# Loading the first weights in halves, and a new order of the steps

## The chip, the cores and the metric

The kernel runs on one core of a Trainium2 chip. The metric is the device time of one execution in microseconds; it is the median of three runs: 506.88 us before the change (506.82 to 507.07). Engines are named as in the profile: PE is TensorE, DVE is VectorE, ACT is ScalarE, POOL is GpSimd, SP is SyncE, which here only issues DMAs.

## The reference

Three layers follow one another. The first is a chunked scan (batch 4, 8 heads, 768 positions, head size 32, state size 16), the second a dense layer with a leaky rectifier, the third a layer of 8 experts, where each token goes to one expert.

```
# scan, per chunk: L = exp(cum_i - cum_j) below the diagonal
y     = (C B^T * L) x + (C state) * exp(cum)
state = exp(sum log a) * state + sum_j B_j x_j exp(cum_end - cum_j)
x = y.transpose(0, 2, 1, 3).reshape(3072, 256)
# dense layer, 256 -> 2048 -> 256
h = x @ w_in;  x = max(0.01 * h, h) @ w_out
# experts: e = argmax(x @ w_gate + bias[modality])
out[mask_e] = softmax_e * (relu(x[mask_e] @ w1[e]) @ w2[e])
```

The weights `w_in` and `w_out` come as 64-bit floats: the kernel reads 8 bytes per element and rebuilds 32-bit floats on the chip.

## The kernel before, in words

The tokens are worked on in 24 chunks of 128 (the scan) and 6 blocks of 512 (the dense layer). Every large product is made of three in the `fp32r` type: the weight's rounded part times the data's rounded part, and the two cross products with the remainders. A *step* is a small function; its name in the plan has the chunk, block or piece as numbers:

- `load.c`, `lx.c`, `le.c`: the DMAs of chunk c. `load` (L419, L420) brings C and B, 1024 pieces of 64 bytes each; `lx` (L428) brings x; `le` (L438) brings the decays back from memory.
- `decay_a`, `decay_b`, `rows`, `high`, `out`, `cr`, `lows`, `lowv`, `end`, `fullmm`, `full`: the *decays' chain*, once, at the start: log of `a`, transposed on PE, summed by a triangular product (L351), copied to `cum` (L353), then laid out in rows.
- `bc.c.q`, `exp.c.q`: the decay matrices of the first chunks by PE and ACT. `trmm`, `trc`, `trb`, `trd`, `trde`, `cb`, `mul`, `p3`, `xa`, `xb`, `st`: the rest of the scan for chunk c: transposes, C times B (L549), times the decays on DVE (L558, L561), times x (L578 to L594), eviction to `xh` on ACT (L609) and its remainder `xl` on DVE (L615), the new state.
- `raw.i.k`, `raw.o.k`: the DMA of a quarter k of `w_in` (L656) or `w_out` (L672), 1 MB each. Each quarter is then converted in two halves: `hb` and `lb` on ACT (L634, L639), `or`, two instructions on DVE (L644, L645), which I call the *pair*, then `cast` on ACT and `subg` or `subv` (remainder) on POOL or DVE (L1188).
- `h.f` (six products, L694) with `sa`, `gg`, `gh`, `gl` on ACT, DVE, ACT, DVE; `y.f` (six products, L736): the dense layer, feature block f. `m1`, `m2`, `m2q` (L1070, L1101) do the same for the experts; `lg`, `l2`, `r1`, `rx`, `r2`, `r3`, `rp`, `be`, `put`, `yr`, `yc`, `ro` choose each token's expert and store rows.
- `warm.c.n`, `wy.n.1`: n products of zeros on PE, whose results are not used. `decay_a` has more of them inside.

The order is written out by hand: `PLAN` is a string of some 1,600 steps, and a loop calls them one by one. Each engine executes its own instructions in the order in which the plan issues them; between engines only data and buffers make an instruction wait. Some buffers that matter: two PSUM banks for `h`, three slots for raw weights, four for each of the chunk's inputs.

[...]

Of the kernel before, what the change touches and what calls it, by code (L numbers as in the profile page):

```python
# [27 lines left out]
    raw.o.0 exp.0.0 lx.0 cb.0 load.3 end high cd.1 bs.0 out warm.1.5 cr mul.0.0 hb.i.0.1 mul.0.2 trmm.1 lows trd.1
    trc.1 fullmm lb.i.0.1 lowv trde.1 or.i.0.1 bc.1.0 trb.1 lb.i.0.0 bc.1.1 exp.1.0 cumd or.i.0.0 lx.1 trmm.2 exp.1.1
    bc.2.0 full lx.2 cb.1 mul.0.1 cast.i.0.0 bs.1 cd.2 bc.2.1 cast.i.0.1 trc.2 subg.i.0.0 mul.1.1 p3.0 load.4 mul.1.0  # L30
    exp.2.1 mul.1.2 trb.2 subv.i.0.1 trd.2 xa.0 cb.2 cd.3 exp.2.0 st.0 le.4 trde.2 bc.3.1 bs.2 raw.i.1 xb.0 hb.o.0.0
    trmm.3 mul.2.1 lx.3 p3.1 mul.2.0 trb.3 hb.o.0.1 trc.3 load.5 mul.2.2 bc.3.0 xa.1 lb.o.0.0 st.1 trd.3 trde.3 xb.1
    or.o.0.0 exp.3.1 p3.2 exp.3.0 bs.3 cb.3 cast.o.0.0 cd.4 st.2 trmm.4 xa.2 mul.3.1 subg.o.0.0 wy.4.1 lb.o.0.1
    mul.3.0 trc.4 le.5 xb.2 trb.4 mask.4 mul.3.2 load.6 trd.4 trde.4 hb.i.1.0 p3.3 or.o.0.1 exp.4.0 xa.3 cd.5 trmm.5
    exp.4.1 xb.3 le.6 st.3 h.0 lx.4 lb.i.1.0 trc.5 raw.o.1 bs.4 mask.5 trb.5 cast.o.0.1 load.7 trd.5 h.1 sa.0 or.i.1.0
    trde.5 exp.5.0 cb.4 subv.o.0.1 sa.1 cast.i.1.0 gg.0 mask.6 hb.i.1.1 mul.4.2 h.2 lb.i.1.1 mul.4.0 subg.i.1.0
    mul.4.1 gh.0 gg.1 trmm.6 exp.5.1 p3.4 or.i.1.1 le.7 h.3 lx.5 xa.4 gl.0 gh.1 lx.6 sa.2 st.4 y.0 trb.6 cast.i.1.1
    trc.6 xb.4 hb.o.1.0 gl.1 sa.3 cb.5 bs.5 load.8 subv.i.1.1 exp.6.0 y.1 gg.2 mask.7 mul.5.0 gh.2 mul.5.1 load.9 h.4
    mul.5.2 lb.o.1.0 gl.2 exp.6.1 gg.3 p3.5 raw.i.2 or.o.1.0 gh.3 le.8 y.2 xa.5 le.9 sa.4 bs.6 lx.7 exp.7.0 cd.7 xb.5
    h.5 load.10 gl.3 gg.4 cb.6 sa.5 cast.o.1.0 y.3 mul.6.0 hb.o.1.1 gg.5 subg.o.1.0 gh.4 mul.6.1 trmm.7 mul.6.2  # L40
    lb.o.1.1 h.6 gh.5 gl.4 trb.7 or.o.1.1 exp.7.1 p3.6 sa.6 trc.7 h.7 bs.7 le.10 xa.6 gg.6 cast.o.1.1 raw.o.2 st.6
# [1247 lines left out]
```

## Time and profile before

| | us |
|---|---|
| median of three runs | 506.88 |
| the profiled execution, its own time | 507.78 |
| its span | 506.0 |
| PE busy | 491.9 (97%) |
| DVE busy | 324.3 (64%) |
| ACT busy | 284.9 (56%) |
| POOL busy | 130.4 (26%) |

The scan and the first two blocks of the dense layer begin together; the dense layer's products start at 31 us, the experts' products at 356 us, and the last product ends just before 499 us. The span of the profile is shorter than the execution's own time by 1.8 us, which lie around it. PE is "busy" while any product is in flight, so a busy PE can still lose time between products; starts of products tell more than the busy share.

### The profile page before, as it was taken

How to read it: one execution, taken by the hardware profiler on the slowest of the kernel's cores; microseconds unless marked ns; L12 is line 12 of the kernel's file. 1: busy time of each engine (PE TensorE's matmuls, PEld its weight loads, DVE VectorE, ACT ScalarE, POOL GpSimd, SP SyncE). 2: the span in 40 equal slices, each digit the busy share in tenths (PEclk: the TensorE clock that was granted, in tenths of full speed). 3: DMA queues.
4: the chain of work that ended last, by engine and by line, in shares of the span. 5: the costliest groups of instructions: out<-in, count | busy, mean ns of one | idle time of the engine just before them, and what ended most of it. 6: DMA issues, size and time to landing. Idle time of an engine off the chain costs nothing.

```text
span 506.0 us, 8845 instructions
## 1 busy us (share of the span) xinstructions
PE 491.9 (97%) x3250; PEld 392.2 (78%) x3252; DVE 324.3 (64%) x702; ACT 284.9 (56%) x627; POOL 130.4 (26%) x131
## 2 busy tenths in 40 slices
PE   8889999999999999999999999999999999999994
PEld 5556787776777777777777778788899989989894
DVE  3999989978768666676667854577772536335330
ACT  6898878855556735564566434654543564354331
POOL 2140215100040302030101103072035448063054
PEclk9999999999999999999999999999999999999998
DMA  8999860051626096136200271018026746050012
GB/s 196 200 214 230 249 157 2 1 88 22 122 54 107 1 101 130 47 25 135 78 1 2 47 258 44 0 29 120 23 40 149 251 147 218 35 169 2 0 59 74
DMA packets 102454, 48.40 MB, mean 96 GB/s; under 512 B 84065, under 2 KB 93698, under 8 KB 102402
## 3 DMA queue, kind: packets, MB, share of 16 engines
q1 hardware_dynamic: 99330, 41.35, 36.8%
q0 software_dynamic: 3072, 6.41, 4.1%
q8 instruction: 27, 0.44, 0.4%
q14 instruction: 25, 0.20, 0.1%
HBM read 41.14 MB, written 6.60 MB: 94 GB/s over the span
## 4 chain that ended last, share of the span: by engine, by line
PE 63%; issue 17%; POOL 7%; DVE 4%; DMA 4%; ACT 4%; POOLq 1%; SPq 0%; ACTq 0%
PE y L736 25%; PE h L694 25%; POOL out_dram L1131 4%; PE cb L549 2%; PE psy L591 2%; POOL w2s L1044 2%; DMA il<-ids,pi 2%; POOL xg L1022 1%; PE psy L586 1%; DMA xt<-in_x_dram 1%; PE hp L1070 1%; ACT e L460 1%; DVE gl L716 1%; PE yr L897 1%; PE lp L779 1%
## 5 line engine op out<-in xcount | busy, mean ns | idle before, releaser
L701 ACT ACTIVATE sa<-h 128x512 f32<-128x512 f32 x96 | 57.5, 598 | 58.8 <-PE h L694 58.6
L706 DVE TENSOR_TENSOR gg<-sa,h 128x512 f32<-128x512 f32 x96 | 65.2, 681 | 26.2 <-ACT sa L701 25.6
L694 PE MATMUL h<-xh,wih 128*128 128x512 f32 x192 | 79.1, 412 | 1.7 <-ACT xh L609 0.9
L716 DVE TENSOR_TENSOR gl<-gg,gh 128x512 fp32r<-128x512 f32 x96 | 67.1, 702 | 19.8 <-ACT gh L711 18.4
L736 PE MATMUL y<-gh,woh 128*128 128x512 f32 x192 | 79.2, 412 | 0.0
L736 PE MATMUL y<-gl,woh 128*128 128x512 f32 x192 | 75.3, 392 | 0.2
L694 PE MATMUL h<-xl,wih 128*128 128x512 f32 x192 | 75.2, 392 | 0.0
L736 PE MATMUL y<-gh,wol 128*128 128x512 f32 x192 | 75.1, 391 | 0.0
L694 PE MATMUL h<-xh,wil 128*128 128x512 f32 x192 | 75.0, 391 | 0.0
L711 ACT CAST gh<-gg 128x512 fp32r<-128x512 f32 x96 | 59.1, 619 | 21.5 <-DVE gg L706 18.2
L1088 DVE SCALAR_TENSOR_TENSOR hl<-hp,hh 128x512 fp32r<-128x512 f32 x48 | 33.1, 690 | 58.4 <-ACT hh L1084 58.4
L1101 PE MATMUL o<-w2s,hh 128*128 128x256 f32 x384 | 70.3, 282 | 0.0
L1070 PE MATMUL hp<-x2h,w1s 128*128 128x512 f32 x192 | 67.3, 396 | 0.1
L1101 PEld LDWEIGHTS o<-w2s,hh 128*128 128x128 f32 x384 | 61.8, 190 | 3.1
L1084 ACT ACTIVATE hh<-hp 128x512 fp32r<-128x512 f32 x48 | 28.6, 599 | 61.3 <-PE hp L1070 51.8
L1101 PE MATMUL o<-w2s,hl 128*128 128x256 f32 x192 | 54.1, 282 | 0.0
L460 ACT ACTIVATE e<-e,ncum 128x128 f32<-128x128 f32 x160 | 50.8, 397 | 0.0
L442 POOL TENSOR_SCALAR_AFFINE_SELECT e<-e 128x1024 f32<-128x1024 f32 x20 | 22.9, 1150 | 102.4 <-DMA e<-cumd 78.0
L694 PEld LDWEIGHTS h<-xh,wih 128*128 128x128 f32 x192 | 36.2, 188 | 15.5 <-issue 3.6
L880 POOL DMA_INDIRECT il<-ids,pi x24 | 25.9, 1077 | 81.6 <-DVE base L871 59.0
L736 PEld LDWEIGHTS y<-gh,woh 128*128 128x128 f32 x192 | 36.1, 188 | 10.6 <-issue 3.3
L694 PEld LDWEIGHTS h<-xh,wil 128*128 128x128 f32 x192 | 36.0, 188 | 7.9
(227 smaller groups left out, 805.2 us busy)
## 6 DMA issues: line engine op xcount, KB each, us to landing
r<-in_moe_w_dram SPq DMA_DIRECT2D x24, 512.0 KB, 4.8
e<-cumd SPq DMA_DIRECT2D x20, 512.0 KB, 4.4
raw<-in_moe_w_in_dram SPq DMA_DIRECT2D x4, 1024.0 KB, 6.2
raw<-in_moe_w_out_dram SPq DMA_DIRECT2D x4, 1024.0 KB, 6.5
...
ct<-in_C_dram SPq DMA_DIRECT2D x24, 64.0 KB, 4.8
bt<-in_B_dram SPq DMA_DIRECT2D x24, 64.0 KB, 3.8
```

Of the source, the lines that this page charges most:

```text
L460: s.activation(out=e[:, h, :], in_=i, func=AF.Exp, bias=ncum[:, cc, b * H + h:b * H + h + 1])
L694: t_.matmul(h, lhsT=w[:, k, fs], rhs=xx[:, k, :], start=(i == 0), stop=(i == 5))
L701: s.activation(out=d["sa"], in_=d["h"], func=AF.Copy, scale=0.01)
L706: v.tensor_tensor(out=d["gg"], in0=d["sa"], in1=d["h"], op=ALU.max)
L711: s.copy(out=d["gh"], in_=d["gg"])
L716: v.tensor_tensor(out=gl, in0=d["gg"], in1=d["gh"].bitcast(F32), op=ALU.subtract)
L736: t_.matmul(y_t[j][k], lhsT=w[:, f, ds], rhs=gg, start=(f in first and i == 0), stop=(f in last and i == 2))
L880: w = g.indirect_dma_start(out=il[:], out_offset=IndirectOffsetOnAxis(ap=pi[:, q:q + 1], axis=0), in_=ids[:, c0 + q:c0 + q + 1], in_offset ...
L1070: t_.matmul(d["hp", f], lhsT=d[1][:, k, part, fs], rhs=xx[:, k, :], start=(n == 0), stop=(n == 5))
L1084: s.activation(out=e_h(i, f, "hh"), in_=ex[i]["hp", f], func=AF.Relu)
L1088: v.scalar_tensor_tensor(out=e_h(i, f, "hl"), in0=d["hp", f], scalar=0.0, in1=d["hh", f].bitcast(F32), op0=ALU.max, op1=ALU.subtract)
L1101: t_.matmul(d["o", q], lhsT=d[h, f][:, q * P:(q + 1) * P], rhs=d[2][:, f, part, :], start=(start and n == 0), stop=(f == NF2 - 1 and n == ...
```

## The change

1. A quarter of a weight is loaded by two DMAs of 512 KB in place of one of 1 MB: `raw.i.k.kk` brings 128 of 256 rows, `raw.o.k.q` half of the rows. The buffer is still one for both halves. There are 16 such DMAs in place of 8. The first half of `w_in`'s first quarter is issued straight behind `a`, ahead of the first chunk's C and B.
2. Products of zeros: the three in `decay_a` (L355, 256 columns) and the five of `warm.1.5` (512 columns) go; `wy.4.1` behind the transposes of chunk 4 becomes `wy.6.1`. Twelve such products become six (the six at the very start and the two at L346 and L347 stay).
3. The plan is in another order from end to end. It has the same steps otherwise.

```diff
 PLAN = """
-    load.0 raw.i.0 kg1 load.1 decay_a kvb bc.0.1 kvc decay_b bc.0.0 exp.0.1 load.2 trmm.0 hb.i.0.0 rows trc.0 trb.0
+    raw.i.0.0 load.0 kg1 load.1 decay_a hb.i.0.0 bc.0.1 load.2 lb.i.0.0 decay_b kvb bc.0.0 exp.0.1 kvc or.i.0.0
...
@@ def decay_a():
         v.tensor_copy(cum.rearrange("p c r -> p (c r)"), p1[:, 0:NCB * BH])
-        for _ in range(3):
-            t_.matmul(p0[:, 256:512], lhsT=zer[:, 0:P], rhs=zer[:, 0:256], start=True, stop=True)
         dk["cum"] = cum
...
-    def load_win(k):
-        r = rawp.tile([P, 2, 512], w_in.dtype, tag="raw", name="raw")
-        nc.sync.dma_start(out=r, in_=w_in[:, k * 512:(k + 1) * 512].rearrange("(k p) f -> p k f", p=P))
-        raws["i", k] = r
+    def load_win(k, kk):
+        if kk == 0:
+            raws["i", k] = rawp.tile([P, 2, 512], w_in.dtype, tag="raw", name="raw")
+        nc.sync.dma_start(out=raws["i", k][:, kk, :], in_=w_in[kk * P:(kk + 1) * P, k * 512:(k + 1) * 512])
...
-    def load_wout(k):
-        r = rawp.tile([P, 4, DM], w_out.dtype, tag="raw", name="raw")
-        nc.sync.dma_start(out=r, in_=w_out[k * 512:(k + 1) * 512, :].rearrange("(k p) f -> p k f", p=P))
-        raws["o", k] = r
+    def load_wout(k, q):
+        if q == 0:
+            raws["o", k] = rawp.tile([P, 4, DM], w_out.dtype, tag="raw", name="raw")
+        o = k * 512 + 2 * q * P
+        nc.sync.dma_start(out=raws["o", k][:, 2 * q:2 * q + 2, :], in_=w_out[o:o + 2 * P, :].rearrange("(k p) f -> p k f", p=P))
```

What this moves on the engines is shown at two places. First SP, from its first DMA on (`ct` and `bt` are C and B of a chunk, `xt` is x). Before:

```order
L1157 DMA a_sb<-in_a_dram 96x256
L419 DMA ct<-in_C_dram 128x8x16
L420 DMA bt<-in_B_dram 128x8x16
L656 DMA raw<-in_moe_w_in_dram 128x2x512
L419 DMA ct<-in_C_dram 128x8x16
L420 DMA bt<-in_B_dram 128x8x16
L419 DMA ct<-in_C_dram 128x8x16
L420 DMA bt<-in_B_dram 128x8x16
L672 DMA raw<-in_moe_w_out_dram 128x4x256
L428 DMA xt<-in_x_dram 128x8x32
```

After:

```order
L1157 DMA a_sb<-in_a_dram 96x256
L656 DMA raw<-in_moe_w_in_dram 128x512
L418 DMA ct<-in_C_dram 128x8x16
L419 DMA bt<-in_B_dram 128x8x16
L418 DMA ct<-in_C_dram 128x8x16
L419 DMA bt<-in_B_dram 128x8x16
L418 DMA ct<-in_C_dram 128x8x16
L419 DMA bt<-in_B_dram 128x8x16
L656 DMA raw<-in_moe_w_in_dram 128x512
L418 DMA ct<-in_C_dram 128x8x16
L419 DMA bt<-in_B_dram 128x8x16
L673 DMA raw<-in_moe_w_out_dram 128x2x256
```

The first half quarter of `w_in` now stands ahead of all chunks' C and B, the second half behind those of three chunks; half a quarter of `w_out` stands where a whole one stood.

Second DVE, behind the copy of `cum` and some constants (`hb<-hb,lb` and `hb<-raw,hb` are the pair of a half quarter; `cumb` is the last step of the decays' chain that `bc.1` waits for). Before:

```order
L496 TENSOR_TENSOR cm<-ps,par 128x256
L400 COPY cend<-p__264 32x2
L400 COPY cend<-p_251 32x4
L450 TENSOR_TENSOR cd<-ct,ecum 128x128
L538 TENSOR_TENSOR bs<-bt,e 128x128
L380 TENSOR_TENSOR cr<-p_251,cumb 64x512
L558 TENSOR_TENSOR e<-e,cb 128x256
L561 TENSOR_TENSOR e<-e,cb 128x512
L496 TENSOR_TENSOR cm<-ps,par 128x256
L387 TENSOR_TENSOR cumb<-cr,cumb 32x512
L644 SCALAR_TENSOR_TENSOR hb<-hb,lb 128x512
L645 SCALAR_TENSOR_TENSOR hb<-raw,hb 128x512
```

After:

```order
L643 SCALAR_TENSOR_TENSOR hb<-hb,lb 128x512
L644 SCALAR_TENSOR_TENSOR hb<-raw,hb 128x512
L495 TENSOR_TENSOR cm<-ps,par 128x256
L537 TENSOR_TENSOR bs<-bt,e 128x128
L449 TENSOR_TENSOR cd<-ct,ecum 128x128
L399 COPY cend<-p__274 32x2
L399 COPY cend<-p_261 32x4
L379 TENSOR_TENSOR cr<-p_261,cumb 64x512
L557 TENSOR_TENSOR e<-e,cb 128x256
L449 TENSOR_TENSOR cd<-ct,ecum 128x128
L557 TENSOR_TENSOR e<-e,cb 128x256
L386 TENSOR_TENSOR cumb<-cr,cumb 32x512
```

The pair of the first half stands ahead of chunk 0's `cm` now. Before, two pairs followed the instruction that writes `cumb`, one behind the other (the first ends the rows shown); after, only one pair stands near that place.

In the dense layer's stretch, from the first `h` to the last `y`, the plan interrupts the `h` and `y` steps with shorter PE steps 77 times in place of 80, with the same 102 short steps.

## Rows read from the trace of the kernel before

**Rows 1.** Section 1 of the page: busy time, share, instructions.

```profile
PE 491.9 (97%) x3250; PEld 392.2 (78%) x3252; DVE 324.3 (64%) x702; ACT 284.9 (56%) x627; POOL 130.4 (26%) x131
```

**Rows 2.** Busy us (count) of PE, PEld, DVE, ACT, POOL by stretch; granted clock, DMA share, GB/s.

```profile
0.00:10.00 10.00, 8.61 (x56) 5.83 (x59) 3.16 (x14) 5.41 (x11) 3.59 (x18) 1.00 0.80 158
...
20.00:30.00 10.00, 8.84 (x117) 5.35 (x118) 9.45 (x26) 7.82 (x21) 2.45 (x2) 1.00 0.99 242
30.00:40.00 10.00, 8.95 (x65) 6.04 (x66) 9.17 (x20) 10.00 (x30) 3.79 (x3) 1.00 0.95 238
...
50.00:75.00 25.00, 25.00 (x165) 19.45 (x166) 21.79 (x40) 20.69 (x47) 4.18 (x3) 1.00 0.75 216
```

**Rows 3.** PE's waits: total us, times, longest.

```profile
PE h L694 <- DVE gg L706: 0.9, 3, 0.4
...
PE rp L849 <- DVE ohb L827: 0.6, 1, 0.6
PE yr L897 <- ACT cdt L529: 0.4, 1, 0.4
```

**Rows 4.** Timeline of the opening: start, duration, instruction [idle before <- what ended it].

```profile
1.27 0.42 SPq L419 DMA_DIRECT2D ct<-in_C_dram  x1
...
4.87 0.21 ACT L341 ACTIVATE tab<-tab 1x8 f32<-1x8 f32 x1
...
6.75 0.28 DVE L273 TENSOR_TENSOR gm<-mask 128x128 f32<-128x128 f32 x1
...
9.09 0.69 ACT L634 ACTIVATE hb<-raw 128x512 f32<-128x512 f32 x1
...
9.39 0.42 DVE L496 TENSOR_TENSOR cm<-ps,par 128x256 f32<-128x256 f32 x1 [2.20 <-PE ps L491]
...
15.19 0.69 DVE L644 SCALAR_TENSOR_TENSOR hb<-hb,lb 128x512 int32<-128x512 int32 x1
```

**Rows 5.** Section 6 of the page: DMA issues, size, median us to landing.

```profile
raw<-in_moe_w_in_dram SPq DMA_DIRECT2D x4, 1024.0 KB, 6.2
...
ct<-in_C_dram SPq DMA_DIRECT2D x24, 64.0 KB, 4.8
```

**Rows 6.** Timeline, products of zeros and what stands behind them.

```profile
1.27 2.74 PE L1153 MATMUL wps<-zer 128*128 128x512 bf16 x6 [1.27 <-DVE tab L1150]
...
5.64 0.85 PE L355 MATMUL p<-zer 128*128 128x256 bf16 x3
...
11.48 1.03 PE L1165 MATMUL bc<-zer 128*128 128x512 bf16 x4 [0.16 <-issue]
...
13.44 0.33 PE L490 MATMUL ps<-ident,ct 128*128 128x128 f32 x1 [0.93 <-DVE e L558]
```

**Rows 7.** Timeline ahead of the first product of the dense layer.

```profile
30.82 0.36 ACT L609 CAST xh<-psy 128x256 fp32r<-128x256 f32 x1
...
31.23 0.50 PE L694 MATMUL h<-xh,wih 128*128 128x512 f32 x1 [0.88 <-ACT xh L609]
```

**Rows 8.** Timeline, a short step inside the dense layer's stream.

```profile
270.33 0.39 PE L736 MATMUL y<-gh,wol 128*128 128x512 f32 x1
270.65 0.71 PE L549 MATMUL cb<-cm,btt 32*128 32x256 f32 x8
271.29 0.50 PE L694 MATMUL h<-xh,wih 128*128 128x512 f32 x1
271.63 0.40 PE L694 MATMUL h<-xl,wih 128*128 128x512 f32 x1
```

**Rows 9.** Timeline, a stall inside the stream.

```profile
232.26 1.09 POOL L442 TENSOR_SCALAR_AFFINE_SELECT e<-e 128x1024 f32<-128x1024 f32 x1 [10.23 <-PE psy L594]
...
233.42 0.39 PE L736 MATMUL y<-gh,wol 128*128 128x512 f32 x1
...
234.21 0.50 PE L694 MATMUL h<-xh,wih 128*128 128x512 f32 x1 [0.41 <-DVE gg L706]
```

**Rows 10.** One line of DVE: count, ns min/median/max, first and last start us.

```profile
L835 DVE TENSOR_SCALAR sm<-sm x6: 170/170/906, 145.1 to 365.6; 128x4 f32<-128x4 f32 x6
```

More of the change, by code (lines that the diff above doesn't have):

```diff
@@ L26 @@
 PLAN = """
-    load.0 raw.i.0 kg1 load.1 decay_a kvb bc.0.1 kvc decay_b bc.0.0 exp.0.1 load.2 trmm.0 hb.i.0.0 rows trc.0 trb.0
[L28 to L41, printed above, removed]
@@ L117 @@
-    m1.5.2 re.5.1 rl.5.1 m2.4.5 re.5.2 rl.5.2 m1.5.3 m1.5.4 re.5.3 oe.3.1 rl.5.3 re.5.4 m1.5.5 sh2.5.0 rl.5.4 m2.4.6
-    oe.3.0 re.5.5 sc.3.0 rl.5.5 m1.5.6 sl2.5.0 sc.3.1 m1.5.7 re.5.6 sc.3.2 rl.5.6 m2.4.7 re.5.7 sc.3.3 rl.5.7 oe.4.2
-    m2q.5.0 oe.4.3 oe.4.1 oe.4.0 sc.4.0 m2q.5.1 sc.4.1 sc.4.2 m2q.5.2 sc.4.3 oe.5.1 oe.5.0 sc.5.0 sc.5.1 m2q.5.3
-    oe.5.2 sc.5.2 oe.5.3 sc.5.3
+    raw.i.0.0 load.0 kg1 load.1 decay_a hb.i.0.0 bc.0.1 load.2 lb.i.0.0 decay_b kvb bc.0.0 exp.0.1 kvc or.i.0.0
+    raw.i.0.1 trmm.0 exp.0.0 load.3 rows trc.0 trb.0 cast.i.0.0 bs.0 cd.1 subg.i.0.0 cb.0 end high raw.o.0.0 out cr
@@ new lines @@
+    lx.0 mul.0.0 lows fullmm cd.2 mul.0.1 hb.i.0.1 cumd lowv trmm.1 lx.1 full trd.1 trc.1 lb.i.0.1 bc.1.0 mul.0.2
+    trde.1 bc.1.1 or.i.0.1 trb.1 exp.1.0 trmm.2 raw.o.0.1 exp.1.1 cb.1 lx.2 trc.2 hb.o.0.0 bc.2.1 bs.1 cd.3 trb.2
+    mul.1.0 lb.o.0.0 trd.2 mul.1.2 p3.0 exp.2.1 load.4 or.o.0.0 cast.i.0.1 bc.2.0 xa.0 trde.2 xb.0 bc.3.1 exp.2.0
+    mul.1.1 subv.i.0.1 cast.o.0.0 trmm.3 cb.2 st.0 exp.3.1 le.4 bs.2 subg.o.0.0 trc.3 hb.o.0.1 lx.3 p3.1 mul.2.0 trb.3
+    mul.2.2 raw.i.1.0 mul.2.1 bc.3.0 xa.1 load.5 xb.1 trd.3 exp.3.0 cb.3 st.1 trde.3 bs.3 p3.2 cd.4 lb.o.0.1 mul.3.2
@@ new lines @@
+    mul.5.2 h.4 mask.7 sa.3 mul.5.0 gh.2 gg.3 lx.7 exp.6.1 p3.5 gl.2 cd.7 lx.8 h.5 xa.5 gh.3 xb.5 exp.7.1 load.9 bs.6
+    gl.3 cb.6 sa.4 y.2 mul.6.1 lb.o.1.0 mul.6.0 le.8 mul.6.2 sa.5 raw.o.1.1 trmm.7 gg.4 load.10 y.3 trb.7 exp.7.0
+    trc.7 or.o.1.0 p3.6 gg.5 trd.7 xa.6 h.6 gh.4 xb.6 trde.7 st.6 cast.o.1.0 bs.7 gl.4 raw.i.2.0 cb.7 gh.5 le.9
+    subg.o.1.0 h.7 raw.i.2.1 mul.7.2 hb.o.1.1 raw.o.2.0 mul.7.1 lb.o.1.1 gl.5 le.10 y.4 sa.6 raw.o.2.1 mul.7.0
+    or.o.1.1 sa.7 load.11 p3.7 gg.7 trmm.8 gg.6 xa.7 y.5 cast.o.1.1 xb.7 gh.6 subv.o.1.1 h.16 gl.6 gh.7 cd.8 gl.7
@@ new lines @@
+    te1 yr.3.1 xb.21 y.69 gl.70 yc.3.1 sa.71 sa.72 gg.71 cb.22 gg.72 gh.71 y.70 mul.22.0 gl.71 r3.3 h.73 gh.72
+    mul.22.2 mul.22.1 y.71 gl.72 sa.73 te2 yr.3.0 h.74 yc.3.0 gg.73 ro.3 lx.23 trmm.23 sa.74 p3.22 gh.73 exp.23.0
+    gl.73 y.72 st.22 trb.23 xa.22 gg.74 h.75 trc.23 gh.74 te3 y.73 sa.75 gl.74 ix.0 h.76 gg.75 w1.0 trd.23 sa.76 y.74
+    ix.1 trde.23 gh.75 gg.76 w2.0 xb.22 h.77 gh.76 bs.23 gl.75 cb.23 sa.77 h.78 gg.77 gl.76 mul.23.0 y.75 sa.78
+    mul.23.1 gg.78 h.79 mul.23.2 p3.23 sa.79 gh.77 y.76 ga.1 xa.23 xb.23 gl.77 h.80 gh.78 gl.78 y.77 gg.79 sa.80 gg.80
@@ L121 @@
+    m2.4.5 re.5.3 dr sl2.5.1 rl.5.3 m1.5.4 m1.5.5 re.5.4 rl.5.4 m2.4.6 re.5.5 rl.5.5 m1.5.6 m1.5.7 re.5.6 rl.5.6
+    m2.4.7 re.5.7 rl.5.7 oe.4.2 m2q.5.0 oe.4.0 oe.4.1 sc.4.0 sc.4.1 m2q.5.1 oe.5.0 oe.4.3 sc.4.2 sc.4.3 m2q.5.2 oe.5.1
+    sc.5.0 sc.5.1 m2q.5.3 oe.5.2 sc.5.2 oe.5.3 sc.5.3
 """
@@ L1202 @@
         "trde": tr_de, "cb": cb_mm, "bs": cb_bs, "mul": cb_mul, "p3": p3_mm, "xa": p3_xa, "xb": p3_xb, "st": p3_st,
-        "raw": lambda t, k: (load_win if t == "i" else load_wout)(k),
+        "raw": lambda t, k, q: (load_win if t == "i" else load_wout)(k, q),
         "h": lambda f: h_mm(f // NF, f % NF), "sa": lambda f: h_sa(f // NF, f % NF), "gg": lambda f: h_gg(f // NF, f % NF),
```

150 lines of the change are left out of this document (75 added, 75 removed).

## The prediction

> **What bounds the kernel now.** I read the busy times first, then the same by stretch, then PE's waits, then the timeline where the waits are. PE is busy for 491.9 us of the span of 506.0 [rows 1], and from 50 us on it fills every stretch, while DVE and ACT still have time over [rows 2]. So whatever the change does behind 50 us can only come from PE's own sequence: how closely product follows product. The opening is different. Between 20 and 40 us DVE is busy for 9.45 and 9.17 of each 10 us and ACT for 10.00 of the second ten, while PE loses more than one microsecond in each [rows 2]. PE then waits 0.88 us for ACT's `xh` (from 30.82 us) before the first dense product, which starts at 31.23 us [rows 7]. So the opening ends when DVE and ACT have worked through their lists; the DMA queue is full beside them (share 0.99 from 20 to 30 us), but no wait of PE ends on a landing there. What the kernel can win is bounded: the opening, the waits inside PE's stream, and the joints between products.
>
> **The change part by part.** The number of products, evictions and conversions is the same but for the zeros, so I price places.
>
> *The first pair in an idle place.* Before, DVE stands idle for 2.20 us ahead of chunk 0's `cm` at 9.39 us, from the end of the constants at 7.2 us on (9.39 - 2.20; the last row before it begins at 6.75) [rows 4]. The pair of `w_in`'s first half ran at 15.19 us, at 0.69 us an instruction, so 2 x 0.69 = 1.38 us, in the stretch that DVE fills. The change puts it into the idle place. Can the data be there? Its DMA is issued second, in the place where C of chunk 0 stood, at 1.27 us [rows 4]. A full megabyte takes 6.2 us to land [rows 5] and a half cannot take longer in an emptier queue, so it lands by 7.5 us; half the 6.2 gives 4.4 us. ACT needs `hb` and `lb`, 0.69 us each by the row of `hb` (1.4 us), and has nothing else from 5.08 us on (4.87 plus 0.21) but the exponential of `cum`, until the first decay matrix is there [rows 4]. The pair can then begin between 6.5 and 9.3 us. At the early end it is done before `cm` could start; at the late end it delays `cm` by 1.3 us, which takes all of the gain back. I take the early end, since by the rows DMA serves half a megabyte first. DVE's list ahead of the first dense product is then 1.38 us shorter, and ACT's by the same 1.4 us: -1.4 us. If PE's part of the opening moves too (next paragraph), at most 0.8 more: -2.2.
>
> *Behind the half.* Chunk 0's C and B now stand behind 512 KB. They took 4.8 us to land in a loaded queue [rows 5]; another 1.6 us, a quarter of 6.2, brings them to 8 us at the latest, and the transposes that read them end at about 9.4 us [rows 4]. I cost it at nothing; if that cover is gone, each microsecond of lateness is one on the chain. The scan's loads behind it gain, since half a quarter of `w_out` and half of `w_in` stand ahead of x of chunk 3 where whole ones stood. SP issues eight DMAs more; with the DMA engines at 0.99 [rows 2] it is the queue and not SP that sets the pace: nothing.
>
> *The zeros.* The three at L355 take 0.85 us on PE ahead of the first decay matrix, 0.64 us of it start to start (0.21 each) [rows 6]. The five of `warm` fill a time in which PE waits anyway: behind them it is still idle for 0.93 us until DVE has the first product ready [rows 6]. Their removal is worth nothing. The two added ones cost 2 x 0.22 = 0.43 us, by the row of the four at 11.48 us (1.03 us less the last one's flight of 0.38, over three); they stand behind chunk 4's transposes, where DVE's list is the limit. Both ends: -0.64 (the chain moves up by all three) to +0.43. I take 0 and leave both ends in the range.
>
> *Joints.* In the stream a product follows the last after 0.23 us. Around one short step the row before it and the row behind it start later: 270.65 - 270.33 = 0.32, 271.63 - 271.29 = 0.34 [rows 8], so 0.09 + 0.11 = 0.2 us for each interruption. Three fewer: -0.6 us (-0.3 to -0.9, as the kinds of steps differ).
>
> *Waits inside the stream.* PE waits 0.9 us in three places for `gg`, 0.6 for `rp` and 0.4 for `yr`: 1.9 us in five places [rows 3]. The starts lose more than the idle time shows: 234.21 - 233.42 = 0.79 where 0.23 is the pace, so 0.56 against 0.41 idle [rows 9]. With 0.15 more for each of five: 1.9 + 0.75 = 2.65 us. The row in front explains the one at 234.21: DVE's L835 on 4 numbers took 906 ns once and 170 ns otherwise [rows 10], and in that time POOL ran an affine select, 1.09 us from 232.26 [rows 9]. Such a delay hits PE only where the plan leaves `gg` little time. A `y` has six or more large steps between it and its `h` in 43 of 96 cases, in the old order in 37: a little more room. I expect a third of the 2.65 back, -0.9 us, with ends -2.65 (all gone) and +1.0 (all stay, and two more of 0.5).
>
> The Trainium skill, SBUF — State Buffer, section "Who interferes with whom", says that GpSimd and VectorE hold a shared pair of ports exclusively, whoever came first, and that a plain `tensor_scalar` can be among them. The 906 ns agree with it. By that rule the waits are tied to the number of such meetings, and POOL has the same instructions as before; then this term is 0, the sum -2.0 and the time 504.9.
>
> Sum: -1.4 - 0.6 - 0.9 = -2.9 us. The profiled execution took 507.78 us (its span of 506.0 and 1.8 around it) and would take 504.9; it stands 0.90 above the median of the three runs, and from that median, 506.88, I get **504.0 us**. The low end adds -2.2 - 0.9 - 2.65 = -5.75: 501.1. The high end, +0.43 - 0.3 + 1.0 = +1.1: 508.0. What lies behind the last product I leave as it is: the last steps are the same.
>
> **The rivals.**
>
> *The gain of the opening is swallowed.* Behind 31 us ACT is full for ten microseconds (10.00 of 10 [rows 2]); if the dense layer's start is early but its evictions come no earlier, PE waits there instead. For it: ACT's row. Against: ACT's list is shorter by the same 1.4 us. The time: joints alone, 506.88 - 0.6 = 506.3.
>
> *PE's clock.* In the opening the six first zero products start about 0.43 us apart ((2.74 - 0.58) / 5, taking 0.58 as the last one's flight), the three at 5.64 us with half the columns 0.21; at 11.48 us the full ones start 0.22 apart [rows 6]. So PE rises from 1.2 to 2.4 GHz between 6 and 11 us, after an unbroken run of products since 1.27 us; the column of the granted clock reads 1.00 all the time and does not show it [rows 2]. If without the three zeros the rise fails to come in the opening's first part, the decay matrices, rows and transposes take twice as long: between the zeros that end at 6.49 and those at 11.48 us lie 5.0 us [rows 6], at the busy share of 0.86 [rows 2] 4.3 us of work. Then the first term is +4.3 in place of -1.4: +4.3 - 0.6 - 0.9 = +2.8, 509.7. Each microsecond at the lower level costs half a microsecond, so it decides over the 2.9 us of the forecast if the rise comes later than 6.5 + 2 x 2.9 = 12.3 us. Against: the decay matrices move up into the zeros' place and keep PE as busy. The Trainium skill, TensorE: Matmul & The Clock Gate, section "Part 1: The HAM clock gate (the "warmup" mystery)", says that the slow state is the default, that activity lifts it, and that where the rise falls varies from run to run. It speaks against taking products of zeros out, and the rise in the rows agrees with it.
>
> *The waits stay.* The order of before is good already and the new one has as many meetings of POOL and DVE: -1.4 - 0.6 = -2.0, 504.9. It lies inside the forecast's own side.
>
> *New waits.* If the new order has twice as many (+2.65) and the half lands late (0): 506.88 + 2.65 - 0.6 = 508.9.
>
> **How the numbers follow.** Two tenths of a percent, 1.0 us, is about what a measurement can tell from no change here. Forecast (faster, 501 to 505.8, the waits that stay among it): 0.70. Swallowed (506.3, no change): 0.16. Clock: 0.07. New waits: 0.07, of both together 0.13 slower and 0.01 about the same. So faster 0.70, same 0.17, slower 0.13. The range is 501.2 to 507.2: it leaves the two slower rivals out, about 0.13, and little below.
>
> **What would show it.** In the new profile the first pair (`hb` on DVE) stands between 6.5 and 9 us and `cm` starts no later than 9.5; the first dense product starts at 29.8, not 31.2 (29.0 to 31.6); PE's waits for `gg`, `rp` and `yr` sum to 1.3 or less; from the first dense product to the last expert product it takes some 1.5 us less than before. I am wrong if the first dense product stays at 31, if the first decay matrices' products start at twice their distance beyond 8 us, or if PE's waits inside the stream are 2 us or more.

## The result and the profile after

The changed kernel takes 511.05 us (median of 5 runs, 509.49 to 511.34) where the kernel before takes 506.88 (505.93 to 507.68). The ratio is 1.0074, with a 95% interval of 1.0060 to 1.0088: slower by some 3.8 us by the ratio, where I had predicted 504.0. The profiled execution took 510.19 us, with a span of 508.5 us (before: 507.78 and 506.0). It lies 0.9 us below its median and the one of before 0.9 above, so the two traces show only 2.4 of the 4.2 us between the medians.

The place to begin is the same as before: how busy TensorE is. Section 1 of the page of the changed kernel:

```profile
PE 491.9 (97%) x3246; PEld 393.5 (77%) x3246; DVE 332.4 (65%) x702; ACT 285.7 (56%) x627; POOL 131.3 (26%) x131
```

PE's record has four instructions fewer and is busy for the same 491.9 us [rows 1]; a product that runs slowly counts as busy too. DVE has the same 702 instructions, and they take 8.1 us more in all. Both say: look at the waits and at durations that have changed. PE's waits in the changed kernel (us in total, times, longest):

```profile
PE psy L590 <- DMA xt<-in_x_dram: 2.6, 1, 2.6
...
PE l L793 <- DVE lt L786: 1.1, 1, 1.1
...
PE o L1101 <- DVE hl L1088: 0.7, 1, 0.7
```

The waits for `gg`, `rp` and `yr`, 1.9 us in [rows 3], are gone, and these three stand in their place. The timeline of the changed kernel shows the opening, and then the first of the three:

```profile
5.62 0.67 ACT L633 ACTIVATE hb<-raw 128x512 f32<-128x512 f32 x1 [0.54 <-DMA raw<-in_moe_w_in_dram]
...
7.03 0.68 DVE L643 SCALAR_TENSOR_TENSOR hb<-hb,lb 128x512 int32<-128x512 int32 x1
...
8.35 0.42 DVE L495 TENSOR_TENSOR cm<-ps,par 128x256 f32<-128x256 f32 x1
...
29.86 0.48 PE L694 MATMUL h<-xh,wih 128*128 128x512 f32 x1
...
147.75 0.37 SPq L419 DMA_DIRECT2D bt<-in_B_dram  x1
...
148.17 5.52 SPq L427 DMA_DIRECT2D xt<-in_x_dram  x2
...
161.13 0.64 PE L590 MATMUL psy<-e,xt 128*32 128x128 f32 x16 [2.58 <-DMA xt<-in_x_dram]
...
162.67 0.63 PE L694 MATMUL h<-xl,wih 128*128 128x512 f32 x1
...
163.09 0.63 PE L694 MATMUL h<-xh,wil 128*128 128x512 f32 x1
```

The opening did what was forecast: the first pair runs on DVE at 7.03 us, `cm` follows at 8.35, and the first dense product starts at 29.86 us instead of 31.23 [rows 7]. Much later, x of chunk 13 is issued at 148.17 us (the first of the two `xt` of that row), behind a load of B that SP issues only at 147.75, and it lands 12.8 us later; PE stands still for 2.58 us. Behind that wait the products follow each other at 0.42 us (163.09 - 162.67) instead of 0.23. The reason is the granted clock, the share of 2.4 GHz that PE gets: the column behind the five engines in the same kernel's busy times by stretch.

```profile
12.00:14.00 2.00, 1.69 (x6) 0.80 (x7) 1.94 (x6) 1.78 (x4) 0.00 (x0) 0.53 0.66 129
14.00:16.00 2.00, 2.00 (x17) 1.28 (x15) 1.85 (x3) 1.48 (x5) 0.00 (x0) 0.62 1.12 289
...
160.00:162.00 2.00, 0.87 (x26) 0.79 (x27) 0.02 (x1) 0.00 (x0) 0.00 (x0) 1.00 0.66 154
162.00:164.00 2.00, 2.00 (x14) 1.63 (x13) 1.30 (x4) 1.67 (x5) 0.00 (x0) 0.57 0.99 183
164.00:166.00 2.00, 2.00 (x7) 1.59 (x6) 1.79 (x10) 1.22 (x2) 0.00 (x0) 0.57 0.97 271
```

From 162.3 to 165.7 us PE runs at 1.2 GHz, just behind a pause; so the late load costs its 2.6 us and about 1.6 more in this trace. From 12 to 16 us the clock is low too, where the zero products stood before.

The other two waits are on DVE. Its line L1044 makes the *remainders* of the expert weights, what the rounded parts leave over. First before, then the changed kernel (ns min/median/max), then the single ones that were stretched:

```profile
L1044 DVE TENSOR_TENSOR w1s<-r,w1s x12: 1206/1218/1292, 334.6 to 466.7; 128x1024 fp32r<-128x1024 f32 x12
```

```profile
L1044 DVE TENSOR_TENSOR w1s<-r,w1s x12: 1214/1221/4128, 330.3 to 464.7; 128x1024 fp32r<-128x1024 f32 x12
...
L1044 POOL TENSOR_TENSOR w2s<-r,w2s x6: 2392/2408/2423, 359.3 to 485.1; 128x1024 fp32r<-128x1024 f32 x6
```

```profile
359.34 2.39 POOL L1044 TENSOR_TENSOR w2s<-r,w2s 128x1024 fp32r<-128x1024 f32 x1 [25.09 <-ACT w2s L1040]
359.62 3.19 DVE L1044 TENSOR_TENSOR w1s<-r,w1s 128x1024 fp32r<-128x1024 f32 x1
...
401.15 4.13 DVE L1044 TENSOR_TENSOR w1s<-r,w1s 128x1024 fp32r<-128x1024 f32 x1
401.76 2.42 POOL L1044 TENSOR_TENSOR w2s<-r,w2s 128x1024 fp32r<-128x1024 f32 x1
...
450.06 3.83 DVE L1044 TENSOR_TENSOR w1s<-r,w1s 128x1024 fp32r<-128x1024 f32 x1 [0.25 <-ACT w1s L1040]
450.38 2.42 POOL L1044 TENSOR_TENSOR w2s<-r,w2s 128x1024 fp32r<-128x1024 f32 x1
```

Three of these twelve run while GpSimd works on the same line, and each takes about its 1.22 us and the time the two lie beside each other; GpSimd's keep their 2.4 us. In the kernel before no two of them meet. `lt` and `hl` stand in DVE's list behind the first two, and PE waits for them; behind the third nothing waits.

The last place is the end. From the start of the last group of products to the end of the span it was 10.1 us before and is 11.3 now, and the program's last waits on GpSimd (L1235) spread out. First the changed kernel, then the one before (first and last start in us):

```profile
L1235 POOLq EVENT_SEMAPHORE  x5: 17/43/43, 504.1 to 506.4; - x5
```

```profile
L1235 POOLq EVENT_SEMAPHORE  x5: 17/43/43, 502.7 to 503.0; - x5
```

The five waits began within 0.3 us of each other and now begin within 2.3: GpSimd pauses for 2.1 us among them (504.2 to 506.3 us), and in that pause a load on a queue of instructions runs, at 504.7 us.

Starts of the same work in the two traces and in four kernels below (timeline, us):

| start of | before | changed | x13_early | lows_apart | splice140 | x13_dve |
|---|---|---|---|---|---|---|
| first dense product | 31.23 | 29.86 | 31.55 | 31.95 | 30.43 | 29.77 |
| dense product `h`, block 2, step 0 | 140.82 | 136.35 | 138.14 | 138.53 | 138.37 | 136.57 |
| block 4, step 0 | 251.40 | 249.61 | 247.20 | 251.51 | 249.56 | 245.93 |
| last dense step | 357.90 | 356.83 | 354.43 | 358.74 | 356.10 | 353.15 |
| expert slot 3 | 424.97 | 426.30 | 423.72 | 425.85 | 423.17 | 420.83 |
| last product group | 495.85 | 497.17 | 494.59 | 496.71 | 494.05 | 491.69 |
| end of the span | 505.98 | 508.47 | 506.16 | 508.65 | 503.98 | 501.83 |

The changed kernel is 4.47 us ahead at 141 us, and 2.49 behind at the end. It loses 2.7 us between 141 and 251, 0.7 to 358, 2.4 to 425 and 1.2 in the tail (each is the change of the difference between the two columns).

### The profile page after: what moved, and what is told of

The parts are those of the page before. It is cut to its first block, busy times and chain, and to the rows that moved or that the text cites. A ratio compares the mean times of both kernels' runs of the same rounds, so it can differ in the third digit from the quotient of the medians.

```text
span 508.5 us, 8885 instructions
## 1 busy us (share of the span) xinstructions
PE 491.9 (97%) x3246; PEld 393.5 (77%) x3246; DVE 332.4 (65%) x702; ACT 285.7 (56%) x627; POOL 131.3 (26%) x131
## 4 chain that ended last, share of the span: by engine, by line
PE 83%; issue 4%; DMA 3%; DVE 3%; SPq 2%; POOL 1%; ACT 1%; POOLq 0%; DVEq 0%
PE y L736 26%; PE h L694 25%; PE hp L1070 11%; PE o L1101 10%; PE psy L590 3%; DMA xt<-in_x_dram 3%; PE cb L548 2%; POOL out_dram L1131 1%; PE psy L585 1%; PE yr L897 1%; DVE w1s L1044 1%; PE xps L1051 1%; SPq L418 1%; DMA cumd<-cumrow 1%; PE lp L779 1%
## 5 line engine op out<-in xcount | busy, mean ns | idle before, releaser
L716 DVE TENSOR_TENSOR gl<-gg,gh 128x512 fp32r<-128x512 f32 x96 | 68.6, 717 | 14.6 <-ACT gh L711 13.8
L441 POOL TENSOR_SCALAR_AFFINE_SELECT e<-e 128x1024 f32<-128x1024 f32 x20 | 24.4, 1228 | 110.3 <-DMA e<-cumd 75.8
L694 PEld LDWEIGHTS h<-xh,wih 128*128 128x128 f32 x192 | 36.4, 189 | 10.4 <-issue 2.5
```

The costliest lines, as they stand in the source:

```text
L694: t_.matmul(h, lhsT=w[:, k, fs], rhs=xx[:, k, :], start=(i == 0), stop=(i == 5))
L716: v.tensor_tensor(out=gl, in0=d["gg"], in1=d["gh"].bitcast(F32), op=ALU.subtract)
```

## The experiments

Each group of runs had its own runs of the kernel before: 506.8, 509.4, 506.7, 509.8 and 510.0 us. So the ratio to these counts; one thousandth is half a microsecond. The changed kernel has 1.0074 from its first runs, with which the first two groups are compared. In the third group (put0_late, which turned out to be the same order) it had 1.0090, in the fifth (pair_after) 1.0128: the loss itself differs from group to group, by more than the smaller steps below.

**First group (506.8): one suspect each.**

x13_early. The load goes back to where it stood before, which is 131.58 us in this trace (131.98 before):

```diff
- ... l2.1 gh.34 y.33 lx.13 gl.34 ...
+ ... p3.10 ... load.15 trc.11 st.10 lx.13 trb.11 ...
```

> The changed kernel with one load moved: x of chunk 13 is issued where the kernel before issues it, right behind the store of chunk 10, and no longer behind the bias-table load that waits for chunk 13's decays. Theory A (the late load costs the 2.66 us that the product psy of chunk 13 waits for xt, and the 1.6 us that the dense products behind it lose at 1.2 GHz): the kernel takes 511.05 - 4.2 = 506.8 us (506.0 to 507.8), no wait of psy on xt above 0.3 us, and the granted clock stays at 1.00 from 155 to 170 us. Rival B (the queue is slow there while the lists are scattered, so another transfer that lands between 144 and 160 us takes the place of x): 510 to 511 us, with a wait of 1.5 us or more on another DMA between 150 and 175 us.

Measured: 507.43 us, ratio 1.0010 (0.9995 to 1.0025), against the change's 1.0074: 3.2 us. No wait for `xt` is left, and the clock stays up:

```profile
162.00:164.00 2.00, 2.00 (x11) 1.58 (x9) 1.29 (x4) 1.66 (x5) 0.00 (x0) 1.00 0.46 98
164.00:166.00 2.00, 2.00 (x12) 1.71 (x11) 1.79 (x10) 1.59 (x3) 0.00 (x0) 1.00 1.05 174
```

Between 141 and 251 us this kernel gains 1.5 us on the one before where the changed one loses 2.7: 4.2 us, as theory A says. The late load is the largest single loss of the first group. (The bias-table load of the expectation is the load of B of chunk 17, which SP holds back until DVE is done with chunk 13's `bs`.)

lows_apart:

```diff
- ... sl1.1.1 lg.5 re.0.1 ... lt.5 ... rl.0.3 r3.5 ...
+ ... lg.5 re.0.1 ... lt.5 ... rl.0.3 sl1.1.1 r3.5 ...
- ... m1.1.7 sl1.2.0 sl2.2.1 ... m2.1.7 sc.0.3 ...
+ ... m1.1.7 sl1.2.0 sc.0.3 sl2.2.1 ... m2.1.7 ...
```

> The changed kernel with VectorE's and GpSimd's remainders of the expert weights taken apart at two places: the second remainder of w1 of expert slot 1 goes behind the fourth hl of slot 0 (it ran beside a GpSimd remainder from 359.6 us and took 3.19 us), and the scatter of the last rows of slot 0 goes ahead of the second GpSimd remainder of slot 2's w2 (VectorE's w1s beside it took 4.13 us from 401.15 us). Theory A (VectorE stands still while GpSimd's remainder runs, and TensorE waits for what is behind it: 1.1 to 1.3 us at lt and 0.9 us at hl): every w1s takes 1.2 to 1.8 us, both waits fall below 0.3 us, and the kernel takes 511.05 - 2.1 = 509.0 us (508.4 to 509.8). Rival B (the waits are the order's, not the remainders': lt and hl come late for another reason): the durations fall, the waits stay at 0.7 us or more, and the time stays within 0.5 us of 511.05.

Measured: 508.99 us, ratio 1.0040 (1.0024 to 1.0055): 1.7 us less than 1.0074. Both waits are gone, and between 358 and 425 us the kernel keeps its place (+0.84 to +0.88 against before) where the changed one loses 2.4. The two remainders take 1.2 us again; the third, of 3.85 us, is left where nothing waits, so that part of the expectation was wrong. Theory A holds.

zeros_back (three products back in the decays' chain, `warm.1.5` ahead of `trmm.1`):

> The changed kernel with zero products back in the opening: three of 256 columns in the decays' chain, as before, and five of 512 columns ahead of the second chunk's mask products. Theory A (TensorE's fall to 1.2 GHz from 12 to 15 us delays the opening: the slow products there cost 0.6 + 0.6 + 0.2 us): the granted clock stays above 0.95 from 10 to 16 us, the first dense product starts 0.7 to 1.4 us earlier than 29.86, and the kernel gains as much (509.7 to 510.4 us). Rival B (VectorE's list is what bounds the opening, so TensorE's clock there is hidden): the clock stays up, the first dense product starts at 29.5 to 30.2 us and the kernel takes 511.0 us (510.6 to 511.4). Rival C (the zeros themselves stand in the way, 0.5 to 1 us): 511.5 to 512.1 us.

Measured: 509.55 us (507.34 to 512.37), ratio 1.0068 (1.0040 to 1.0095). The clock reads 1.00 from 10 to 18 us and the first dense product starts at 28.92 us, as in theory A. The time settles nothing: four executions lie between 507.3 and 508.3 us and four between 510.8 and 512.4. The profile is the fastest of them; there PE waits only 1.2 us for `xt`, and the clock does not fall behind it.

splice140 (the changed order up to `y.15`, at 108 us, and behind it the tokens that are left in the order of before):

> The changed kernel's first 140 us (its order up to the second product of block 15, loads in halves, zeros as changed) and behind it the rest in the order of the kernel before. Theory A (the change is good up to there and its loss of 8.6 us lies in the order of the rest): the second product of block 15 starts 4.4 us earlier than in the kernel before and the end keeps it: 506.88 - 4.4 = 502.5 us (501.5 to 503.5). Rival B (what is won early is waited away in any order, because a transfer or the routing sets the pace behind 140 us): 505.5 to 507 us, with a new wait of 2 us or more between 140 and 250 us.

Measured: 505.44 us (503.18 to 506.79), ratio 0.9969 (0.9951 to 0.9986): 1.6 us faster than before, so the opening's order is good and the loss lies in the rest. The 4.4 us were not reached. In its profile the clock is low from 12 to 19 us and the first dense product starts at 30.43; from there to 141 us it gains 1.65 us on the kernel before, where the changed kernel gains 3.1.

**Second group (509.4): sums, zeros, GpSimd's program.**

> The changed kernel with all three edits of the runs before at once: x of chunk 13 early, VectorE's and GpSimd's remainders apart at both places, and the eight zero products back in the opening. Theory A (three separate losses, so they add): 3.2 us for the load by its ratio, 1.7 for the remainders by theirs, and 1 to 2 us because TensorE then keeps 2.4 GHz from 12 to 19 us, out of 511.05: 504.7 us (503.0 to 505.7), the mean granted clock at 0.993 or more in all executions, and no wait of TensorE inside the stream of dense products above 0.6 us. Rival B (TensorE is not what bounds the first 60 us, so one of the gains covers another): 506 to 507.5 us.

All three repairs at once (the early load, the remainders apart, the zeros) give 511.68 us, ratio 1.0033 (1.0013 to 1.0053). The profiled execution, the fastest of its twelve, was 3.4 us ahead of the before trace at the last dense step, as hoped, and only 0.7 at expert slot 3: near 400 us PE pauses several times with no wait in the record (`issue`, 1.5 us in two lines). Neither theory named that; see the last group.

> The spliced kernel (the changed order up to 108 us, behind it the order before) with the eight zero products back in the opening. Its executions without them ranged from 503.2 to 506.8 us with mean granted clocks from 0.996 down to 0.989. Theory A (that spread and some 2 us of its median are the fall to 1.2 GHz between 12 and 19 us): with the zeros the clock stays up, the first dense product starts at 28.5 to 29.5 us instead of 30.43, and the time is 503.5 us (502.5 to 504.5), with the executions within 2 us of each other. Rival B (VectorE's list sets the opening): 505.0 to 505.8 us, as without the zeros, whatever the clock does.

Measured: 507.15 us (506.17 to 508.55), ratio 0.9951 (0.9934 to 0.9969), faster than the kernel before. The executions lie within 2.4 us, with mean clocks of 0.993 or more. The first dense product is at 30.39 us, no earlier than without zeros; so A is right on the clock and the spread, and B on the start in this one profile.

before_nozeros (the kernel before with the changed kernel's zero products: eight go, two are added):

```diff
-        for _ in range(3):
+        for _ in range(0):
- warm.1.5 ... wy.4.1
+ wy.6.1
```

> The kernel before with the changed kernel's zero products and nothing else of the change: the three of the decays' chain and the five ahead of the second chunk's mask products are left out, and six instead of four stand behind the fourth chunk. Theory A (the zeros keep TensorE at 2.4 GHz in the opening): the clock falls between 11 and 20 us, the first dense product starts 0.7 to 2.5 us later than 31.23, and the kernel takes 507.5 to 509.3 us. Rival B (VectorE bounds the opening, and the chunks' products have room): the clock falls and the first dense product stays within 0.5 us of 31.23; 506.4 to 507.2 us. Rival C (the zeros were in the way): 505.3 to 506.3 us.

Measured: 511.00 us, ratio 1.0034 (1.0016 to 1.0051), so 1.7 us slower than before. The first dense product starts at 32.94 us, 1.7 later than in the before trace. Theory A:

```profile
10.00:12.00 2.00, 0.55 (x8) 0.15 (x8) 1.05 (x5) 2.00 (x6) 0.00 (x0) 1.00 0.83 213
12.00:14.00 2.00, 1.33 (x7) 1.17 (x8) 1.93 (x5) 1.54 (x4) 0.00 (x0) 0.79 1.08 335
14.00:16.00 2.00, 2.00 (x10) 1.43 (x11) 1.93 (x4) 1.12 (x4) 0.00 (x0) 0.50 0.87 105
```

PE is busy for 0.55 us of the two from 10 to 12, since it waits 2.1 us for `e`; then the clock falls and stays at half to 20 us. The zeros filled that wait and were worth 1.7 us here, though nothing reads them. The Trainium skill, TensorE: Matmul & The Clock Gate, section "Part 1: The HAM clock gate (the "warmup" mystery)", says that the default state is throttled and that activity releases the throttle; this trace agrees with it, and so does the low clock behind the wait at 160 us. In before_pool6 below, which has all its zeros, the clock is at half from 14.9 to 18.3 us all the same: they do not hold it every time.

before_pool6 (the kernel before and six idle memsets on GpSimd at about 290 us):

> The kernel before with six small GpSimd memsets added at about 290 us, where GpSimd is idle: they make its program six instructions longer, as the changed kernel's is by its record (311 GpSimd records against 305), and do nothing else. In the changed kernel GpSimd stands still for 2.1 us behind the last scatter, until a code load has come (from 504.2 to 506.3 us), and the time from the last product's end to the end of the span is 8.3 us against 7.2 before. Theory A (a longer program puts a boundary of GpSimd's code there): a pause of 2 us or more in GpSimd's record behind the last scatter, 8.3 to 9.0 us from the last product to the end, and 507.9 to 508.7 us. Rival B (the pause comes from the order of the last scatters or waits): no pause, 7.0 to 7.3 us, 506.8 us (506.4 to 507.2).

Measured: 511.65 us, ratio 1.0040 (1.0025 to 1.0056), 2.0 us slower. GpSimd's last waits (L1235), here and then in before_nozeros, which has as many GpSimd instructions as the kernel before, in the same group:

```profile
L1235 POOLq EVENT_SEMAPHORE  x5: 17/43/43, 506.8 to 509.0; - x5
```

```profile
L1235 POOLq EVENT_SEMAPHORE  x5: 17/42/43, 505.4 to 506.3; - x5
```

The pause of 1.9 us is there, and the tail from the last product is 10.4 us against 8.2: theory A. The program is longer by six instructions that stand where GpSimd is idle. The other traces bear it out: in all ten whose record has 310 to 312 GpSimd instructions the first and the last of the five waits lie 2.2 to 2.8 us apart, in all nine with 305 or 299 they lie 0.2 to 1.2 apart.

**Third group (506.7): combinations, and the slow load.**

> The changed kernel with the first two edits (x of chunk 13 early, the remainders apart), without the zero products. Alone they took 3.2 and 1.7 us off the changed kernel by their ratios to the kernel before (1.0010 and 1.0040 against 1.0074); all three edits together gave 1.0033, with a 1.9 us pause of TensorE at 396 us that no wait explains. Theory A (the two losses add, and the pause belongs to that program or its runs): 4.9 us off 511.05, a ratio to the kernel before of 0.998 (0.996 to 1.000), on a chip where that takes 506.9 us 505.9 us (504.9 to 506.9). Rival B (taking both away brings a new wait behind 350 us): a ratio of 1.002 or more, and TensorE idle for 1 us or more between 350 and 410 us.

Measured: 505.12 us, ratio 0.9964 (0.9950 to 0.9978), faster than the kernel before. The two losses add (0.0064 + 0.0034 off 1.0074 would be 0.9976).

x13_dve:

```diff
-        (g if t == 2 and k == 1 else v).tensor_tensor(out=lo, ...)
+        v.tensor_tensor(out=lo, ...)
```

with `lx.13` as in x13_early, and `sl2.2.1` behind `xf.2.1`.

> The changed kernel with x of chunk 13 early, all remainders of the expert weights on VectorE (six move from GpSimd, of 2.4 us there and 1.2 on VectorE), and the second of slot 2's w2 behind the remainders of its rows. GpSimd's program is then six instructions shorter, about what the change made it longer. Theory A (two engines' remainders beside each other are what stretches VectorE's, and the length of GpSimd's program is what makes the pause at the end): no remainder above 1.4 us, no pause of 2 us behind the last scatter, 7.0 to 7.5 us from the last product to the end, and 3.2 + 1.7 + 1.2 us off 511.05: 504.9 us (503.9 to 506.2), a ratio to the kernel before of 0.996. Rival B (7.3 us more on VectorE make the hl of the experts late): the pause goes, but TensorE waits for hl by 1 us or more, and the ratio is 0.999 to 1.004.

Measured: 503.14 us (502.17 to 506.47), ratio 0.9935 (0.9911 to 0.9959), the lowest ratio of all runs. No remainder is above 1.3 us, the last product to the end takes 7.2 us, and PE waits for no `hl`. Its remainders:

```profile
L1044 DVE TENSOR_TENSOR w1s<-r,w1s x12: 1215/1218/1250, 326.6 to 459.2; 128x1024 fp32r<-128x1024 f32 x12
L1044 DVE TENSOR_TENSOR w2s<-r,w2s x12: 1194/1218/1292, 343.4 to 473.6; 128x1024 fp32r<-128x1024 f32 x12
```

> The changed kernel with the load of chunk 13's x left late, and the four scatters of the second block's row lists (issued from 140.4 to 145.4 us, landed 16 us later) moved behind, to just ahead of the next block's at 166 us. Theory A (while these scatters are in flight the other transfers crawl, 9 to 46 GB/s from 146 to 160 us, and that is why x, issued at 148.2 us, lands only at 161.0): x lands by 156 us, TensorE waits for it by at most 0.3 us, and the kernel takes 507 us (506.3 to 508.3). Rival B (the queue crawls because of its own packets, the store of the block's 528 KB of rows and the loads of B and C in pieces of 64 and 128 bytes): x lands at 159 to 161 us again, the wait stays at 2 us or more, and the time at 510.3 to 511.5 us.

Measured: 511.73 us, ratio 1.0090 (1.0064 to 1.0117), and the wait for `xt` is still 1.9 us. That looks like rival B, but the run does not test it. The edit moves the scatters in the plan; GpSimd has no other instruction between the old place and the new one, so it issues them where it did before:

```profile
142.73 1.15 POOL L880 DMA_INDIRECT il<-ids,pi  x1 [0.18 <-POOL e L441]
...
146.74 0.99 POOL L880 DMA_INDIRECT il<-ids,pi  x1 [0.30 <-issue]
...
168.01 0.97 POOL L880 DMA_INDIRECT il<-ids,pi  x1 [20.28 <-DVE base L871]
```

In the changed kernel these rows stand at 140.38, 144.38 and 166.24 us. So this is the changed kernel once more, in the third group, and theory A, that the scatters slow the queue, stays open.

> The kernel before with its eight weight loads each issued as two halves, one right behind the other at the old places, and nothing else of the change. Theory A (the halves by themselves are nothing: one issue more of 0.5 us on SyncE at eight places, the same bytes): the same time as the kernel before within 0.3%, and the first half of w_in reaches ScalarE 1 us or more earlier than the whole did. Rival B (a first half lands early enough that the conversion starts earlier and the first pairs get into VectorE's idle place without another order): 505.5 us or less where the kernel before takes 506.9. Rival C (eight more issues push later loads back): 507.7 us or more.

Measured: 506.73 us, ratio 1.0004 (0.9993 to 1.0014). Theory A by its time: split loads alone are worth nothing. In its trace the first dense product starts at 30.24 us, a microsecond earlier than in the trace of before, with the pairs in their old places.

**Fourth group (509.8).** ro0_behind_x13 (`ro.0`, the store of 528 KB of rows, behind `lx.13`, else the changed kernel):

> The changed kernel with the load of chunk 13's x left late behind the same wait of SyncE, and the store of the second block's rows (yx<-ysb, 528 KB, issued at 142.0 us, landed at 153.2) moved behind it. Theory A (the store's packets fill the DMA engines, so what is issued behind it lands 9 us later or more): x lands by 155 us, TensorE's wait for it falls below 0.4 us, and the kernel takes 507 us (506.3 to 508.5), a ratio to the kernel before of 0.9995 to 1.003. Rival B (x is slow by itself, and by the loads of B and C in pieces of 128 bytes ahead of it): it lands at 158 us or later, the wait stays at 1.5 us or more, and the ratio at 1.006 to 1.009.

Measured: 513.79 us, ratio 1.0063 (1.0032 to 1.0094). The wait for `xt` is gone; PE goes from the step ahead straight on:

```profile
160.06 0.49 PE L585 MATMUL psy<-cdt,st 64*128 64x128 f32 x4
...
160.48 0.64 PE L590 MATMUL psy<-e,xt 128*32 128x128 f32 x16
```

x, issued at 150.17 us, is there by 160.48. So without the store ahead of it the load is not late; by what hour it landed the record doesn't tell. Whether the store alone makes it late is not shown. In the changed kernel the store is in flight together with the four scatters, and 35 of its 512 pieces of some 1 KB take over 1 us, the longest 4.5, where the median is 0.05; here it starts behind the scatters' last piece, and none takes over 0.09. The time does not follow (theory A had 0.9995 to 1.003): PE pauses without a wait near 400 us, 1.7 us in two places.

> The fastest kernel so far (x of chunk 13 early, all remainders on VectorE; ratio 0.9935, executions from 502.2 to 506.5 us with mean granted clocks from 0.999 down to 0.989) with the eight zero products back in the opening. Theory A (the fall to 1.2 GHz in the opening is what spreads its executions and costs 1 to 2 us in most): the clock stays at 2.4 GHz from 10 to 20 us, all executions lie within 2 us, and the ratio is 0.990 to 0.992. Rival B (VectorE's list sets the opening and the zeros only keep the clock): the clock stays up, the first dense product starts at 29 to 30.5 us as without them, and the ratio is 0.993 to 0.995.

Measured: 511.25 us (505.65 to 513.62), ratio 1.0008 (0.9976 to 1.0040). Neither theory: the profile is 3.0 us ahead of the before trace at the last dense step and 2.8 behind at expert slot 3, with 2.6 us of pauses without a wait and half the clock from 402.4 to 405.8 us behind them.

**Fifth group (510.0): the changed kernel and two repairs side by side.**

> The changed kernel itself, once more, beside the two that follow. Theory A (its loss is in its order alone): a ratio to the kernel before of 1.006 to 1.0088, as at first. Rival B (the loss also depends on how the group runs): 1.010 or more, with TensorE pausing for 2 us or more near 400 us.

> The fastest variant so far (x of chunk 13 early, all remainders on VectorE) in one group with the changed kernel. Theory A (three of the changed kernel's losses are taken away: the late x, the stretched remainders, GpSimd's pause at the end): 6 to 7.5 us below the changed kernel of this group, and a ratio to the kernel before of 0.992 to 0.996. Rival B (its 0.9935 was the group's luck): less than 5 us below the changed kernel, a ratio of 0.998 or more.

> That variant with the eight zero products back in the opening, in the same group. Theory A (TensorE's fall to 1.2 GHz from 12 to 19 us costs the changed order 1 to 2 us in most executions): 0.8 to 2 us below the variant without zeros, a clock of 2.4 GHz from 10 to 20 us. Rival B (VectorE's list sets the opening, so the zeros only keep the clock): within 0.6 us of the variant without zeros, or slower.

Measured: the changed kernel 516.46 us, ratio 1.0128 (1.0093 to 1.0163); x13_dve 511.86, 1.0014 (0.9986 to 1.0042); with zeros 511.48, 0.9985 (0.9953 to 1.0018). The changed kernel loses more here than at first (rival B). The repairs still gain 4.6 us on it by medians, 5.8 by ratios, but nothing on the kernel before: by its ratio pair_dve came out as its rival B, so 0.9935 belongs to its group in part. The zeros are worth 1.5 us by ratios, and the intervals overlap: not settled. One thing that makes this group slower for the changed order is in the changed kernel's timeline:

```profile
399.17 0.28 PE L1101 MATMUL o<-w2s,hh 128*128 128x256 f32 x1
...
399.71 0.29 PE L1101 MATMUL o<-w2s,hh 128*128 128x256 f32 x1 [0.26 <-issue]
...
401.14 0.40 PE L1101 MATMUL o<-w2s,hh 128*128 128x256 f32 x2 [1.02 <-issue]
```

PE is held for a microsecond between two products of one group that need nothing new, and behind it the clock is at half from 401.5 to 405.0 us. It happens in the profiles of the changed experts' order in the second, fourth and fifth group, not in those of the first and third. The second group's three profiles with the experts in the order of before (splice_zeros, before_nozeros, before_pool6) don't have it; the fourth and fifth group have no such profile, so whether the order of the experts or the group makes it is not separated. The kernel before is itself some 3 us slower in those three groups. The cause stays open.

## Why the prediction was wrong, point by point

- **The first pair in an idle place**: -1.4 forecast, -1.37 in the profile (29.86). The data was there in time, and the pair ran where I put it. The size is partly luck: of ten profiles with the changed opening and no zeros the first dense product starts between 29.77 and 32.32, the middle at 31.56, so at least half of them gain nothing. The three early ones (29.77 to 30.00) have the low clock for some 3.4 us, the seven late ones (30.43 to 32.32) for some 6.8. With the zeros back (five kernels) the clock stays up and the start lies between 28.92 and 30.63, the middle at 30.09. Nor is the gain the pair's alone: in before_halves, with the old order, the start is at 30.24.
- **The zeros**: I took 0, with +0.43 as the high end, for the new ones. This step failed. I had read that PE waits there anyway and so costed their removal at nothing; what they did in that wait was keep PE busy. Measured in the kernel before: +1.7 us (before_nozeros). My rival on the clock had the mechanism; it placed it before 11 us, where the granted clock reads 1.00, while the fall came at 12.1 us in the changed kernel; and it priced it at 4.3.
- **Behind the half**: "nothing" held for the loads that I followed, those of chunks 0 to 3. The step failed where it stopped: the order moved x of chunk 13 behind a store of 528 KB and behind the load of B of chunk 17, for which SP stands still until DVE has read chunk 13's old one; it is issued 16.2 us later than before (131.98 to 148.17). That is 2.6 us of wait and 1.6 of lower clock in the trace, 3.2 us by x13_early. The cost differs: the wait is 2.6, 2.4 and 1.9 us in three traces with this order (lows_apart and put0_late the other two), each with half the clock behind it, and 1.2 and 0.7 in two (zeros_back, pair_after) where the clock stays up. A listing of SP's order would have shown the move.
- **Joints and waits inside the stream**: -0.6 and -0.9. Up to 141 us the changed kernel gains 3.1 us behind its first dense product, twice the sum of the two; the waits for `gg`, `rp` and `yr` are all gone, not a third. But as a term for the whole stream it was wrong: from the first dense product to the last product group it takes 2.7 us more than before, where I had said 1.5 less, and the three waits shown sum to 4.4 us, past the 2 us that I had named as the sign of being wrong. Of these, 1.1 and 0.7 us came from two engines' remainders beside each other, 1.7 us by lows_apart. I had the mechanism in the prediction, for one row of 906 ns, with the count of GpSimd's instructions as the argument that nothing changes; it is which of them meet that counts. The Trainium skill, SBUF — State Buffer, section "Who interferes with whom", says that only the shared port pair causes contention and that it is an exclusive lock; 4.13 us for a 1.22 us instruction beside one of 2.42 agrees with a lock. That whoever came first holds it, as the prediction has it, the trace does not bear out: at 401.15 and 450.06 us DVE's instruction began first, by 0.61 and 0.32 us, and was the one that was stretched.
- **"What lies behind the last product I leave as it is"** failed by 1.2 us: GpSimd's pause at the end, which six more instructions make in the kernel before (before_pool6, 2.0 us) and which is not there in x13_dve, whose GpSimd has six instructions fewer than the changed kernel's.

The sum of what was missed, late load, remainders, tail and zeros: 3.2 + 1.7 + 1.2 + 1.7 = 7.8 us, less the 1.6 that the stream gained up to 141 us beyond my terms (3.1 - 1.5), 6.2; from the forecast of -2.9 that gives +3.3, and +3.8 was measured. The closeness is partly luck: the terms come from different groups, their intervals are 1 to 2 us wide, and the changed kernel's own loss ran from 1.0074 to 1.0128. The -2.9 holds the opening's -1.4 as the one profile shows it, already without the zeros, so their 1.7 us belongs to the executions with the late start.
